# Turning q and k of four heads together, with their loads, a tile's regions and an order table

## The chip, the cores and the metric

The kernel runs on one core of a Trainium2 chip. Its engines run side by side, each through its own instructions in order: TensorE (PE, with the loading of its stationary operand shown apart as PEld), VectorE (DVE), ScalarE (ACT), GpSimd (POOL), SyncE (SP). Here POOL issues most DMAs, those that turn float32 into bf16 among them, and SP the others. The metric is the device time of one execution in microseconds; three runs of the kernel before give a median of 296.29 us (295.89 to 300.01).

## The reference

Attention with one added to the softmax's denominator, over 8 batches of 12 heads (448 tokens, head width 64), then a soft mixture of experts (8 experts, 4 slots each, hidden width 1024):

```python
scores = scale * np.matmul(q, k.transpose(0, 1, 3, 2))
m = np.max(scores, axis=-1, keepdims=True)
e = np.exp(scores - m)
attn = e / (np.sum(e, axis=-1, keepdims=True) + np.exp(-m) + 1e-09)
x = np.matmul(attn, v)            # then heads side by side: x is (3584, 768)
logits = x @ phi                  # (3584, 32)
d = softmax of logits over the rows;  c = softmax of logits over the 32 slots
slot_input = d.T @ x
slot_out[e] = np.maximum(slot_input[e] @ w1[e], 0) @ w2[e]
out = c @ slot_out
```

## The kernel before

Work goes by pairs of heads: 48 pairs, n = 0 to 47, six to a batch. The 448 rows of a pair's scores are four tiles, i = 0 to 3; the last, of 64 rows, holds both heads. The main loop has a slot s per pair, of two halves (y = 0, 1; hs = 2s + y). The steps, with the letter that the order strings use:

- `load` (L168): DMAs by POOL of q, k (six heads, 336 KB each) or v (two issues) into `nq0`/`nq1` and `nv`.
- T: `T(n)` (L241) turns q and k of a pair: 28 transposes of 64x64, one head in rows 0 to 63 and the other in rows 64 to 127, into a PSUM buffer of pool psB; one copy, by ACT (L263) or DVE (L265), takes it to a tile `qk0` to `qk6`.
- a: `A` (L274) computes scores with queries in the partitions (L285, L304) into psA, and DVE takes row maxima (L287, L307). It runs some pairs ahead.
- `W1` (L310, POOL) lays the negated maxima of three pairs out, `W2` (W, L332, PE) turns them and `W3` (ACT) evacuates them.
- B: `Bk` (L352) computes scores with keys in the partitions (s, L367), adds the maxima (b, L370), and ACT takes the exponentials (L372) into one of the `e2` tiles. The letters behind B0, B1, B2 (`assbba`) are the order in which score, bias and `A`'s score matmuls of the two heads are issued. B3 (L393, L396) is tile 3, whose matmuls use a 64x64 part of the array.
- V: `AV` (L418) multiplies exponentials and v (L433), query tiles 0 to 2; H is the fourth, 8 matmuls of 64 columns of stationary operand each.
- N: `N1` (L440) evacuates this to `ubuf`; M: `N2` (L449) makes the denominators (DVE) and divides (POOL, L466 to L477), into `x0` or `x1` by batch.
- X: `PX(n)` (L491) turns 128 columns of x (L498), ACT evacuates (L504) to `xTa`/`xTb`.
- `V(g)` (L403): POOL brings v of six heads into the layout `vp0`/`vp1` that AV reads (L405 to L408).
- P: steps of `P(b)` (L513) for a finished batch: logits (`l_mm`, L532), maxima, exponentials, slot sums (`s_mm`, L620), at half slots listed in `post`.

Up to slot 2 the order is the string `ramp`; from 3 to 41 it is `order[s % 6]`; from 42 on the code below it. PE, ACT, DVE and POOL run in the order in which these steps are issued. Pool psB has four PSUM buffers (T, B, W2, PX), psA three (A, P), psV one (AV).

One big tile `W` holds the weights. Its first 11 parts stay; the part behind (`R`, `at_`) holds the regions named above and takes the last 40 rows of weights when they are free: `rows_at` (L694) says at which half slot up to which row is loaded. Some rows are brought to DRAM as bf16 earlier (`stage_at`), and SP fetches them. After the last slot POOL also fills `spread` and `own4` (L868 to L875), behind its last row loads.

Of the kernel before, what the change touches and what calls it, by code (L numbers as in the profile page):

```python
# [31 lines left out]
def kernel(  # L32
# [47 lines left out]
    NQK, NE, VPN, NATV = 7, 5, HG * 4 * VS, HG * 4 * D  # L80
    sizes = [("nq0", 2 * NP * S), ("nq1", 2 * NP * S), ("nv", NATV), ("qk6", 2 * S), ("wm1", 512),
             ("qk0", 2 * S), ("qk1", 2 * S), ("qk2", 2 * S), ("wm0", 512), ("xTa", 4 * 512), ("qk3", 2 * S),
             ("vp0", VPN), ("x0", 4 * DD), ("qk4", 2 * S), ("qk5", 2 * S), ("e2", NE * 2 * S), ("e1", S),
             ("vp1", VPN), ("xTb", 2 * 512), ("x1", 4 * DD)]
# [72 lines left out]
    with ExitStack() as at:  # L157
# [9 lines left out]

        def load(g, nm, l0=0, l1=NP):  # L168


            b, h0 = g // 2, (g % 2) * HG
            src = {"q": q, "k": k, "v": v}[nm][b, h0:h0 + HG]
            if nm != "v":
                t = part(f"nq{g % 2}", "qk".index(nm) * NP * S, NP * S).rearrange("p (l x) -> p l x", l=NP)
                x = src.rearrange("(l h) (j t) d -> (h j) l (t d)", h=2, t=7)
                gdma(out=t[:, l0:l1, :], in_=x[:, l0:l1, :])
# [8 lines left out]
        raw = w_tile(10)[:, 0:4 * S].bitcast(F32).rearrange("p (a x) -> p a x", a=2)  # L185
        for a, src in enumerate((q, k)):
            nc.sync.dma_start(out=raw[:, a, :], in_=src[0, 0:2].rearrange("h (j t) d -> (h j) (t d)", t=7))
# [26 lines left out]
        first_qk = [part(f"nq0", a * NP * S, NP * S).rearrange("p (l x) -> p l x", l=NP)[:, 0, :] for a in range(2)]  # L214
        nc.scalar.copy(first_qk[0], raw[:, 0, :])  # L215
        nc.vector.tensor_copy(first_qk[1][:, 0:4 * D], raw[:, 1, 0:4 * D])
        nc.scalar.copy(first_qk[1][:, 4 * D:S], raw[:, 1, 4 * D:S])
# [23 lines left out]
        def T(n):  # L241
            g, pl = divmod(n, NP)
            first = n < NP * NP
            ps = psB.tile([128, 2, S], BF16, tag="b", name="ps_t")

            k0 = [psB.tile([128, 2, S], BF16, tag="b", name="ps_k") for _ in range(2)] if n == 0 else None
            for a in range(2):
                src = nat["qk"[a], g]
                order = [(tok, hl) for tok in range(7) for hl in range(2)]
                if a and n == 0:  # L250
                    order.sort(key=lambda z: kcol(z[1], z[0]))
                for tok, hl in order:
                    c = kcol(hl, tok) if a else (2 * tok if tok < 4 else 2 * tok - 7) * 64
                    r = slice(64 * hl, 64 * hl + 64)
                    o = k0[c // 256][r, 0, c:c + 64] if a and n == 0 else ps[r, a, c:c + 64]
                    nc.tensor.transpose(o, src[r, pl, tok * D:(tok + 1) * D], ident[r, r])  # L256
            t = qk_t[n % NQK]
            if n == 0:
                nc.scalar.copy(t[:, 0, :], ps[:, 0, :])
                nc.vector.tensor_copy(t[:, 1, 0:256], k0[0][:, 0, 0:256])  # L260
                nc.vector.tensor_copy(t[:, 1, 256:S], k0[1][:, 0, 256:S])
            elif first or n % 6 in (0, 3):
                nc.scalar.copy(t, ps)  # L263
            else:
                nc.vector.tensor_copy(t, ps)  # L265
            qkT[n] = t

# [132 lines left out]

        def V(g):  # L403
            t, s = vp[g % 2], nat["v", g]
            nc.gpsimd.tensor_copy(t[:, 0:HG:2, 0:3, 0:D], s[:, 0:HG:2, 1:4, :])  # L405
# [43 lines left out]
        def N2(n):  # L449
# [10 lines left out]
            else:  # L460
# [3 lines left out]
            c = pb * 128  # L464
            rec2 = psm.tile([128, 2], F32, tag="rec2", name="rec2", bufs=3)
            eng.tensor_mul(  # L466
                x[:, 0:3, c:c + 128].rearrange("p i (h d) -> p i h d", h=2),
                u[:, 0:6, 0:D].rearrange("p (i h) d -> p i h d", h=2),
                rec[:, 0:6].rearrange("p (i h) -> p i h", h=2).unsqueeze(3).to_broadcast([128, 3, 2, D]))
            if n == NPAIR - 1:  # L470
# [7 lines left out]
                x[:, 3, c:c + 128].rearrange("p (h d) -> p h d", h=2),  # L478
# [197 lines left out]
        for z in range(3):  # L676
            post.setdefault(2 * NPAIR - 5 + 2 * z, []).append(last[z])
# [11 lines left out]
        for _ in range(22):  # L689
# [4 lines left out]
        rows_at = {77: 3, 83: 7, 85: 12, 89: 17, 91: 20, 92: 24, 93: 26, 95: 27}  # L694
# [15 lines left out]
        wait_loads = []  # L710
        waits = [r for z in stage_at.values() for y in z for r in range(*y)]
        def slot_loads(s):
            g = (s + 10) // 3
            if s == 1 or (s and s % 3 == 2):
                if g < NG:
                    load(g, "q")
                    load(g, "k")
            g = (s + 9) // 3
            if s % 3 == 0 and g - 2 < NG - 1:
                V(g - 2)  # L720
                if s and g - 1 < NG:
                    load(g - 1, "v")

        ramp = ("T0 A A T1 A A W0 T2 A G0 A X0 J0 A B0.0 A B0.1 A A T3 A B0.2 A A T4 C0.3 V0.0 W1 A V0.1 V0.2 A X1 T5 "
                "A B1.0 A K0 Y2 K1 D0 V0.3 H0 C1.1 N0 B1.2 A T6 C1.3 V1.0 V1.1 A B2.0 M0 A T7 B2.1 A V1.2 V1.3 W2 T8 "
                "H1 A N1 B2.2 V2.0 X2 C2.3 Z0 V2.1 M1 K2 ")
        for word in ramp.split():
# [17 lines left out]
            elif op == "N":  # L747
                N1(*arg)
            elif op == "M":
                N2(*arg)  # L750
            elif op == "G":
                V(0)
                load(1, "v")
                ones_in(vp[1], nc.gpsimd)
            elif op == "J":
                for nm in "qk":
                    load(2, nm)
                load_half(0, 0, w_tile(0))
            elif op == "D":
                load_half(0, 1)  # L760
            elif op == "Y":
                load(2, "v")
                if 1 in half_at:
                    load_half(half_at[1], 0, w_tile(half_at[1]))
            elif op == "Z":
                PX(0)
            elif op == "K":
                slot_loads(*arg)
        for s in range(3, NPAIR + 1):
            for y in range(2):  # L770
                hs = 2 * s + y
                if s < NPAIR - 6:
                    for word in order[s % 6][y].split():
# [8 lines left out]
                        elif op == "T":  # L782
                            T(s + 6)
# [6 lines left out]
                        elif op == "X":  # L790
                            PX(s - 2)
# [4 lines left out]
                else:  # L796
# [18 lines left out]
                    else:  # L815
# [3 lines left out]
                        if s < NPAIR:  # L819
                            for i in (0, 1):  # L820
                                AV(s, i, range(3))
                    for f in post.get(hs, ()):
                        f()
                    if y and 0 <= s - 2 < NPAIR - 2:
                        PX(s - 2)
# [12 lines left out]
                if y == 0 and s and s + 1 in firsts:  # L838
                    W1(mg(s + 1))
                if y == 0 and wait_loads:  # L840
                    f, z = wait_loads.pop()
                    f(z)
                if y == 0 and s % 3 == 2 and (s + 1) // 3 < NG:
                    if s == NPAIR - 4:
                        V(NG - 1)
                    if s - 1 in half_at:
                        load_half(half_at[s - 1], 0, w_tile(half_at[s - 1]))
                if y == 0 and s - 1 in stage_at:
                    stage_rows(*stage_at[s - 1][0])
                if y == 0 and s - 2 in half_at:  # L850
                    load_half(half_at[s - 2], 1)
                if y == 0 and s - 2 in stage_at:
                    stage_rows(*stage_at[s - 2][1])
# [3 lines left out]
            if s > 2 and s + 2 in firsts:  # L857
                wait_loads.append((slot_loads, s))
            else:
                slot_loads(s)  # L860
            if 2 * s + 1 in rows_at:

                if 2 * s + 1 == 89:
                    load_rows(7, 9)
                load_rows(rows + 2 * (rows == 7), rows_at[2 * s + 1])
# [200 lines left out]
```

## Time and profile before

| what | value |
|---|---|
| three runs, median (lowest, highest) | 296.29 us (295.89, 300.01) |
| the profiled execution | 295.49 us |
| its span, first to last instruction | 293.7 us |
| PE busy | 270.2 us (92%) |
| DVE busy | 249.7 us (85%) |
| ACT busy | 249.0 us (85%) |
| POOL busy | 196.3 us (67%) |
| chain of waits, PE's share | 77% |
| granted TensorE clock, mean | 0.961 |
| q, k DMAs (336 KB), issue to landing, median | 6.4 and 7.2 us |

Busy time of an engine is that of its instructions with overlaps counted once. Matmuls overlap each other, so what one costs is read from the starts of two groups that follow each other, not from its length. The granted clock is full until the output stage after 265 us.

### The profile page before, as it was taken

The page shows a single profiled execution, that of the slowest core. Times are in us where ns is not written, and L with a number is a line of the kernel's source. Part 1 is how long each engine was busy: PE and PEld are TensorE (multiplying, and loading weights), DVE is VectorE, ACT ScalarE, POOL GpSimd, SP SyncE. Part 2 cuts the span into 40 slices and gives each one's busy share as a digit, 9 for nine tenths or more (in the row PEclk, how much of TensorE's full clock was granted, in tenths as well). Part 3 has the DMA queues.
Part 4 walks back from the last instruction along what each step waited for, and adds up shares of the span by engine and source line. Part 5 has one row for each costly group of instructions (what it writes and reads, how often), then busy time and mean ns, then how long its engine had stood idle before and what let it go on. Part 6 is the DMA issues. An engine that isn't in the chain of part 4 may idle for free.

```text
span 293.7 us, 12399 instructions
## 1 busy us (share of the span) xinstructions
PE 270.2 (92%) x5174; PEld 156.9 (53%) x5174; DVE 249.7 (85%) x581; ACT 249.0 (85%) x559; POOL 196.3 (67%) x391
## 2 busy tenths in 40 slices
PE   5999999999999999999999999999999999995810
PEld 4445555565665566565655665556555556652100
DVE  5999799999999989999999999999999565537920
ACT  4569999999999999999999999999999986337810
POOL 8786677889787978897888879887975823000000
PEclk9999999999999999999999999999999999999555
DMA  7999997999999999999999999999989999809997
GB/s 134 150 148 196 175 145 121 196 185 187 187 192 163 199 177 205 180 193 186 198 176 194 188 185 177 191 181 199 155 132 208 197 210 274 303 4 345 382 444 328
DMA packets 47016, 58.67 MB, mean 200 GB/s; under 512 B 2801, under 2 KB 39921, under 8 KB 46705
## 3 DMA queue, kind: packets, MB, share of 16 engines
q0 software_dynamic: 40304, 42.29, 90.7%
q1 hardware_dynamic: 6656, 15.60, 14.0%
q8 instruction: 40, 0.66, 0.8%
q14 instruction: 16, 0.12, 0.1%
HBM read 89.16 MB, written 15.14 MB: 355 GB/s over the span
## 4 chain that ended last, share of the span: by engine, by line
PE 77%; ACT 8%; DVE 4%; POOL 3%; issue 2%; DMA 1%; DVEq 0%; POOLq 0%; ACTq 0%
PE ps_av L433 16%; PE ps_b L367 10%; PE ps_a L285 10%; PE ps_t L256 8%; PE ps_b L370 7%; PE ps_b L393 4%; PE ps_x L498 4%; PE ps_b L396 3%; ACT W L399 2%; PE ps_s L620 2%; PE ps_o L959 2%; DVE mx L298 2%; PE ps_h L896 2%; PE ps_l L532 2%; PE ps_a L294 2%
## 5 line engine op out<-in xcount | busy, mean ns | idle before, releaser
L287 DVE TENSOR_REDUCE mx<-ps_a 128x1 f32<-128x448 f32 x250 | 139.1, 611 | 3.2 <-PE ps_a L285 2.4
L372 ACT ACTIVATE W<-ps_b 128x448 bf16<-128x448 f32 x250 | 125.0, 576 | 4.1 <-PE ps_b L370 3.3
L285 PE MATMUL ps_a<-W 64*128 64x448 bf16 x250 | 82.7, 354 | 0.0
L433 PEld LDWEIGHTS <-W 128*128 128x128 bf16 (+1 forms) x1536 | 53.9, 100 | 34.9 <-issue 31.1
L433 PE MATMUL ps_av<-W 128*128 128x65 bf16 (+1 forms) x1536 | 70.7, 196 | 0.6 <-ACT ubuf L446 0.6
L367 PE MATMUL ps_b<-W 64*128 64x448 bf16 x250 | 65.8, 355 | 0.0
L370 PE MATMUL ps_b<-mT,sel 64*128 64x448 bf16 x250 | 64.6, 350 | 0.0
L466 POOL TENSOR_TENSOR W<-ubuf,rec 128x384 bf16<-128x384 f32 x44 | 36.5, 829 | 27.5 <-DVE rec L462 14.5
L399 ACT ACTIVATE W<-ps_b 128x448 bf16<-128x448 f32 x86 | 46.5, 580 | 2.3 <-PE ps_b L396 2.0
L256 PEld LDWEIGHTS <-W 64*64 64x64 bf16 x1344 | 26.7, 112 | 17.5 <-issue 14.7
L256 PE MATMUL ps_t<-ident,W 64*64 64x64 bf16 x1330 | 31.2, 197 | 1.4 <-ACT W L215 1.4
L504 ACT CAST W<-ps_x 128x512 bf16<-128x512 f32 x47 | 29.6, 631 | 1.2 <-PE ps_x L498 1.0
L307 DVE TENSOR_REDUCE mx<-ps_a 128x1 f32<-128x448 f32 x48 | 29.6, 616 | 0.6 <-PE ps_a L304 0.6
L114 POOL DMA_DIRECT2D W<-in_moe_w_dram x30 | 22.7, 756 | 7.9 <-PE ps_b L396 7.7
L393 PE MATMUL ps_b<-W 64*64 64x448 bf16 (+1 forms) x134 | 26.8, 368 | 0.3
L285 PEld LDWEIGHTS <-W 64*128 64x128 bf16 x250 | 22.5, 94 | 7.8
L396 PE MATMUL ps_b<-mT,sel 64*64 64x448 bf16 (+1 forms) x134 | 25.4, 357 | 0.1
L370 PEld LDWEIGHTS <-sel 64*128 64x128 bf16 x250 | 20.7, 94 | 8.0 <-issue 2.7
L446 ACT COPY ubuf<-ps_av 128x455 f32<-128x455 f32 x44 | 24.4, 555 | 0.0
L263 ACT COPY W<-ps_t 128x896 bf16<-128x896 bf16 x21 | 19.7, 939 | 5.5 <-PE ps_t L256 5.5
L298 DVE TENSOR_REDUCE mx<-ps_a 128x1 f32<-128x448 f32 x38 | 21.1, 616 | 1.5 <-PE ps_a L294 1.5
L477 POOL TENSOR_TENSOR W<-ubuf,rec 128x128 bf16<-128x128 f32 x44 | 17.5, 398 | 3.7
(156 smaller groups left out, 446.6 us busy)
## 6 DMA issues: line engine op xcount, KB each, us to landing
W<-in_moe_w_dram POOLq DMA_DIRECT2D x24, 768.0 KB, 9.4
W<-in_v_dram POOLq DMA_DIRECT2D x32, 192.0 KB, 6.7
out_dram<-W SPq DMA_DIRECT2D x2, 2688.0 KB, 10.5
W<-in_q_dram POOLq DMA_DIRECT2D x15, 336.0 KB, 6.4
W<-in_k_dram POOLq DMA_DIRECT2D x15, 336.0 KB, 7.2
stage<-in_moe_w_dram POOLq DMA_DIRECT2D x4, 768.0 KB, 9.4
W<-stage SPq DMA_DIRECT2D x4, 576.0 KB, 6.9
out_dram<-W SPq DMA_DIRECT2D x6, 384.0 KB, 3.1
```

The costliest lines, as they stand in the source:

```text
L256: nc.tensor.transpose(o, src[r, pl, tok * D:(tok + 1) * D], ident[r, r])
L285: nc.tensor.matmul(ps[:, 0:S], t[r, 0, i * 128:(i + 1) * 128], t[r, 1, :], start=True, stop=True)
L287: nc.vector.reduce_max(m[:, c:c + 1], ps[:, 0:S], axis=AX.X)
L307: nc.vector.reduce_max(mx[g][:, c:c + 1], ps[:, 0:S], axis=AX.X)
L367: nc.tensor.matmul(pss[hl][:, 0:S], t[rs[hl], 1, cols], t[rs[hl], 0, :], start=True, stop=False)
L370: nc.tensor.matmul(pss[hl][:, 0:S], sel[rs[hl], 2 * pl + hl:2 * pl + hl + 1].to_broadcast([64, 128]), mT[mg(n)][rs[hl], :], start=False, s ...
L372: nc.scalar.activation(e[:, hl, :], pss[hl][:, 0:S], AF.Exp, scale=scale)
L393: nc.tensor.matmul(outs[hl], t[rs[hl], 1, cols], t[rs[hl], 0, :], start=True, stop=False)
L396: nc.tensor.matmul(outs[hl], sel[rs[hl], 2 * pl + hl:2 * pl + hl + 1].to_broadcast([64, m]), mT[mg(n)][rs[hl], :], start=False, stop=True)
L399: nc.scalar.activation(e, p[:, 0:S], AF.Exp, scale=scale)
L433: nc.tensor.matmul(o, eT[n, i, hl][:, qc], vp[g % 2][:, 2 * pl + hl, i, 0:W65], start=(i == 0 and u == 0 and hl == 0) or (u == 3 and i == ...
L466: eng.tensor_mul(x[:, 0:3, c:c + 128].rearrange("p i (h d) -> p i h d", h=2), u[:, 0:6, 0:D].rearrange("p (i h) d -> p i h d", h=2), rec[: ...
```

## The change

Four heads at a time: from pair 6 to pair 45 `T4(j, a)` turns q (a = 0) or k (a = 1) of pairs 2j and 2j + 1 with 14 transposes of 128 partitions x 64 columns, and one copy writes the halves into two neighbouring `qk` tiles, of which there are now eight. `load4(j)` loads q and k of four heads (224 KB each) into `raw`, which holds four pairs' places; the load of j + 2 is issued after j is turned. The pairs hold other heads for this (4m + h and 4m + 2 + h), so v's places, the columns written by `N2` and the time of `PX` (s - 3 instead of s - 2) change with them.

```diff
-    NQK, NE, VPN, NATV = 7, 5, HG * 4 * VS, HG * 4 * D
-    sizes = [("nq0", 2 * NP * S), ("nq1", 2 * NP * S), ("nv", NATV), ("qk6", 2 * S), ("wm1", 512),
...
+    NQK, NE, VPN, NATV = 8, 5, HG * 4 * VS, HG * 4 * D
+    two = lambda i: [(f"qk{i}", 2 * S), (f"qk{i + 1}", 2 * S)]
+    sizes = [("raw", 8 * S), ("wm1", 512)] + two(0) + [("nv", NATV)] + two(2) + [("xTa", 4 * 512), ("wm0", 512)] + \
+            two(4) + [("x0", 4 * DD)] + two(6) + [("free", 2 * S), ("e2", NE * 2 * S), ("e1", S), ("vp0", VPN), ("vp1", VPN),
+                                                  ("xTb", 2 * 512), ("x1", 4 * DD)]
...
+        four = lambda n: PB <= n < NPAIR - 2
+
+        def load4(j):
+            b, m = divmod(j, 3)
+            for a, x in enumerate((q, k)):
+                x = x[b, 4 * m:4 * m + 4].rearrange("(l h) (j t) d -> (h j) l (t d)", h=2, t=7)
+                gdma(out=raw[a][:, 2 * (j % 2):2 * (j % 2) + 2], in_=x)
...
+        def T4(j, a):
+            n = 2 * j
+            turned[j] = turned.get(j, 0) + 1
+            if j > 3 and turned[j] == 2 and j + 2 < NPAIR // 2:
+                wanted.append(j + 2)
+            if not four(n):
+                T(n + a)
+                return
+            ps = psB.tile([128, 2, S], BF16, tag="b", name="ps_t")
+            for tok in range(7):
+                for l in range(2):
+                    c = kcol(l, tok) if a else (2 * tok if tok < 4 else 2 * tok - 7) * 64
+                    nc.tensor.transpose(ps[64 * l:64 * l + 64, :, c:c + 64], raw[a][:, (n + l) % 4, tok * D:(tok + 1) * D],
+                                        ident)
+            cp = nc.scalar.copy if (n + a) % 6 in (0, 3) else nc.vector.tensor_copy
+            o = at_[f"qk{n % NQK}"] + a * S
+            cp(R[:, o:o + 4 * S].rearrange("p (h x) -> p h x", h=2)[:, :, 0:S], ps)
...
+            if g >= 2:
+                runs = [(0, slice(0, 3, 2), slice(0, 2), 0), (1, slice(1, 2), slice(0, 2), 1)]
...
+                for hl, a, c, at in runs:
...
+                    nc.gpsimd.tensor_copy(o[:, :, :, 0:3, 0:D], z[:, :, :, 1 - hl:4 - hl, :])
+                    nc.gpsimd.tensor_copy(o[r, :, :, 3, 0:D], z[r, :, :, 3 * hl, :])
...
-            post.setdefault(2 * NPAIR - 5 + 2 * z, []).append(last[z])
+            post.setdefault(2 * NPAIR - 5 + 2 * z + (z == 0), []).append(last[z])
...
-        rows_at = {77: 3, 83: 7, 85: 12, 89: 17, 91: 20, 92: 24, 93: 26, 95: 27}
+        rows_at = {79: 1, 83: 7, 86: 9, 88: 14, 89: 15, 91: 17, 92: 21, 93: 22, 95: 25}
...
-        order = (("P V2 B0assbba V3 B1sabsba",
-                  "H N B2ssbaba T B3 P V0 V1 X M"),
-                 ("V2 P B0assbba V3 B1saasbb",
-                  "H P N B2assbba T B3 V0 V1 X M"),
-                 ("V2 B0assbba P V3 B1assbba",
-                  "H N B2asasbb B3 T W P V0 V1 M X"),
-                 ("B0assbba P V2 V3 H N B1ssabba T",
-                  "M B2sasbba B3 X V0 P V1"),
-                 ("B0assbba T B1sasbba P V2 V3 H",
-                  "N B2assbab B3 V0 P M X V1"),
-                 ("B0assbba V2 V3 P B1sabsab H N",
-                  "B2ssbaab T B3 P V0 W V1 M X"))
+        order = (("V2 V3 B0asbsba H B1assbba N P",
+                  "Q B2sabsab M X V0 P V1 B3"),
+                 ("B0asbsba V2 V3 B1assbba P K",
+                  "H N P B2sabsab B3 M V0 V1 X"),
+                 ("B0ssabba X V2 V3 B1assbba P H N",
+                  "B2sabsab P W V0 V1 M B3"),
+                 ("B0asbsba V2 B1assbba V3 P",
+                  "H N Q P K X M V0 B2sabsab V1 B3"),
+                 ("B0asbsba V2 B1assbba P V3 H N Q",
+                  "B2sabsab B3 V0 M V1 P X"),
+                 ("V2 B0ssabba V3 B1assbba P H K",
+                  "N B2sabsab P B3 V0 W X V1 M"))
+        px_at = {84: 39, 87: 40, 88: 41, 91: 42, 92: 43, 94: 44, 95: 45}
...
-                "A B1.0 A K0 Y2 K1 D0 V0.3 H0 C1.1 N0 B1.2 A T6 C1.3 V1.0 V1.1 A B2.0 M0 A T7 B2.1 A V1.2 V1.3 W2 T8 "
-                "H1 A N1 B2.2 V2.0 X2 C2.3 Z0 V2.1 M1 K2 ")
+                "A B1.0 A K0 Y2 L4 D0 V0.3 H0 C1.1 N0 B1.2 A Q3.0 C1.3 V1.0 V1.1 A B2.0 M0 A Q3.1 B2.1 A V1.2 V1.3 W2 "
+                "H1 A N1 B2.2 V2.0 X2 C2.3 V2.1 M1 L5 ")
...
+                        elif op == "Q":
+                            T4((s + 6 - s % 2) // 2, 0)
+                        elif op == "K":
+                            T4((s + 4 + s % 2) // 2, 1)
...
-                            PX(s - 2)
+                            PX(s - 3)
...
+                if (c, y) in ((1, 0), (4, 0)) and (s + 2) // 3 < NG:
+                    V((s + 2) // 3)
+                if y == 0:
+                    if s % 3 == 2 and s + 1 in firsts:
+                        W1(mg(s + 1))
+                    if c % 3 == 2 and (s + 4) // 3 < NG:
+                        load((s + 4) // 3, "v")
+                while wanted:
+                    load4(wanted.pop())
```

In the ramp J0 loads with `load4(3)`, L is `load4`, Q is `T4`, and K0 is `V(1)`; Z0 was `PX(0)`. In the order strings Q turns q and K turns k. `c` in the last piece is s % 6. The loads of weight halves move from the middle of a slot to its end. L367, L370, L336, L498, L532, L620 of before are L400, L403, L369, L551, L585, L673 of after; the new transposes are L295.

More of the change, by code (lines that the diff above doesn't have):

```diff
@@ L166 @@
         ubuf = pu.tile([128, 2, 7 * W65], F32, name="ubuf")
+        raw = [R[:, 4 * a * S:4 * (a + 1) * S].rearrange("p (l x) -> p l x", l=4) for a in range(2)]
+        extra = [w_tile(9)[:, a * NP * S:(a + 1) * NP * S].rearrange("p (l x) -> p l x", l=NP) for a in range(2)]
+        four = lambda n: PB <= n < NPAIR - 2
[4 more added lines that the diff above has]
+                gdma(out=raw[a][:, 2 * (j % 2):2 * (j % 2) + 2], in_=x)
+        turned, wanted = {}, []
         def load(g, nm, l0=0, l1=NP):
@@ L182, in load @@
             nat[nm, g] = t
[L185 removed]
+        f32 = w_tile(10)[:, 0:4 * S].bitcast(F32).rearrange("p (a x) -> p a x", a=2)
         for a, src in enumerate((q, k)):
[L187 removed]
+            nc.sync.dma_start(out=f32[:, a, :], in_=src[0, 0:2].rearrange("h (j t) d -> (h j) (t d)", t=7))
         make_identity(nc, ident)
@@ L213 @@
         nc.vector.memset(ones[64:128, 1:2], 0.0)
[L214 to L217, printed above, removed]
+        nc.scalar.copy(raw[0][:, 0, :], f32[:, 0, :])
+        nc.vector.tensor_copy(raw[1][:, 0, 0:4 * D], f32[:, 1, 0:4 * D])
+        nc.scalar.copy(raw[1][:, 0, 4 * D:S], f32[:, 1, 4 * D:S])
         for h in range(2):
@@ L266, in T @@
             qkT[n] = t
+        def T4(j, a):
[15 more added lines that the diff above has]
+            cp(R[:, o:o + 4 * S].rearrange("p (h x) -> p h x", h=2)[:, :, 0:S], ps)
+            for h in range(2):
+                qkT[n + h] = qk_t[(n + h) % NQK]
         firsts = [0, 1] + list(range(3, NPAIR, 3))
@@ L755 @@
             elif op == "J":
-                for nm in "qk":
-                    load(2, nm)
+                load4(3)
                 load_half(0, 0, w_tile(0))
+            elif op == "Q":
+                T4(*arg)
+            elif op == "L":
+                load4(*arg)
             elif op == "D":
@@ L856 @@
                     rows = rows_at[hs]
[L857 to L860, printed above, removed]
             if 2 * s + 1 in rows_at:
-                if 2 * s + 1 == 89:
-                    load_rows(7, 9)
-                load_rows(rows + 2 * (rows == 7), rows_at[2 * s + 1])
+                load_rows(rows, rows_at[2 * s + 1])
                 rows = rows_at[2 * s + 1]
```

76 lines of the change are left out of this document (34 added, 42 removed).

## The prediction

> **What bounds the kernel now.** I read the chain of waits first: TensorE (PE) holds 77% of it, and from 37 to 229 us it is PE work in which the same pieces return every 28.7 us. That is six slots; a slot handles one pair of heads. Next I took the busy time of each engine in one such period (the next one takes 28.82).
>
> ```profile
> core 0: us, PE busy (x) PEld busy (x) DVE busy (x) ACT busy (x) POOL busy (x), PEclk, DMA share, GB/s
> 116.67:145.28 28.61, 28.61 (x604) 17.29 (x598) 27.70 (x65) 27.93 (x66) 24.55 (x49) 1.00 1.16 190
> ```
>
> PE (its weight loads, PEld, run beside it) never rests, and three other engines are close behind. ACT and DVE overlap the ends of their instructions, so their true floor is lower. Three lines of the chain of waits show it, and show POOL:
>
> ```profile
> 11.75 3.19 DVE mx L298 x6
> ...
> 92.02 0.81 POOL W L176
> ...
> 101.72 0.40 POOL W L477
> ```
>
> Six maxima back to back take 3.19, so 0.53 each, not the 0.61 of the groups. A period has 42 maxima (22.3), 4 evacuations of turned q and k on DVE (2.1), 6 denominators (0.31 each, 1.9) and some 1.3 of slot statistics: DVE floor 27.6, or 1.1 us under PE. For ACT the same gives about 26.6 (exponentials stand 0.42 to 0.44 apart). POOL, at 24.6 of 28.7, was the chain itself from 92.0 to 101.7.
>
> PE's prices, from its timeline (start, length, line, count):
>
> ```profile
> 100.01 0.32 PE L433 MATMUL ps_av<-W 128*64 128x65 bf16 x8
> 100.26 0.36 PE L367 MATMUL ps_b<-W 64*128 64x448 bf16 x2
> ...
> 100.94 0.56 PE L256 MATMUL ps_t<-ident,W 64*64 64x64 bf16 x24
> ...
> 101.88 0.35 PE L433 MATMUL ps_av<-W 128*128 128x65 bf16 x6
> 102.62 0.34 PE L336 MATMUL ps_m<-ident,W 128*128 128x128 bf16 x3 [0.39 <-POOL W L314]
> ...
> 103.00 0.39 PE L498 MATMUL ps_x<-ident,W 128*128 128x128 bf16 x4
> 103.23 0.34 PE L433 MATMUL ps_av<-W 128*128 128x65 bf16 x6
> ```
>
> Read starts, not lengths. PX: 4 matmuls of 128 columns in 0.23, 57 ns each, so a column streams in 0.44 ns. A score block (100.26 to 100.94) is three streams of 448 columns, 0.19 each, plus 0.11: that is what a change of the array's tile (128x128, 64x128, 64x64, 128x64) costs. Turn of a pair plus B3, both 64x64: 100.94 to 101.88, 0.94. Elsewhere the two stand alone:
>
> ```profile
> 37.45 0.63 PE L256 MATMUL ps_t<-ident,W 64*64 64x64 bf16 x28
> 38.01 0.36 PE L367 MATMUL ps_b<-W 64*128 64x448 bf16 x1
> ...
> 40.20 0.38 PE L393 MATMUL ps_b<-W 64*64 64x448 bf16 x2
> ...
> 40.70 0.36 PE L433 MATMUL ps_av<-W 128*128 128x65 bf16 x6
> ```
>
> A turn alone costs 0.56 and B3 alone 0.50; next to B3 the turn costs 0.94 - 0.50 = 0.44.
>
> **Turning four heads, on PE.** The instruction order of before has, per period, four turns beside B3 and two alone: 4x0.44 + 2x0.56 = 2.88. The change has 84 instead of 168 transposes per period, each of 128 columns on a 128x64 tile. Unknown is whether two of them, on the two column halves, stream together. The nearest rows say yes: the eight L433 on 128x64 tiles take 0.25 with a tile change of 0.11, 17 ns each for 65 columns that alone need 29. So 42 streams x 57 ns = 2.40, and as only one of the six half-turns has a run of its own (the others join the AV pieces of that tile), 0.11 more: 2.51. But AV pieces that were joined are now apart: 15 runs of 128x128 for 13, +0.22. Sum -0.15 a period; 40 turned pairs are 6.7 periods: **-1.0**. Half as many transposes is thus nearly nothing, since columns, not instructions, are paid. If they streamed singly: 42x57 ns = +2.4 a period, +16.
>
> [...]
>
> **Evacuations.** As many copies as before; in the steady part the same third on ACT. The written tiles lie apart by a stride; no row shows that, the copies of equal size are 0.53 (DVE) and 0.79 (ACT) apart, and I take no difference (0 to +0.1 each, 40 copies, mostly under PE).
>
> **Ramp.** ACT runs without a gap from 24 to 37 us; the timeline of ACT has T7's copy at 29.21 and T8's here:
>
> ```profile
> 35.02 1.01 ACT L263 COPY W<-ps_t 128x896 bf16<-128x896 bf16 x1
> 35.80 1.11 ACT L372 ACTIVATE W<-ps_b 128x448 bf16<-128x448 f32 x2
> ```
>
> T7's copy goes to DVE, T8's leaves the ramp, PX(0) is put off: 2x0.79 + 0.47 = 2.05 less on ACT. DVE has three gaps of 0.4 to 0.6 there, enough for one more copy (0.53), and PE saves T8's 0.56. I take **-1.5**, ends -2.0 and 0.
>
> **POOL and loads.** q and k loads go from 34 issues to 48; in a period from 4 to 6, 2x0.79 = +1.6, POOL 24.6 to 26.2 of 28.7. Bytes and packet sizes stay. Behind them on POOL stand N2 and W1. V (2x0.66 + 2x0.35 = 2.0) now stands at the middle of slots 1 and 4 of six. From there to W1 in slot 2: V 2.0, two issues 1.6, N2 1.5, W1 0.8, together 5.9 for the 4.8 of a slot. V may start ahead of its place (it waits for no PE work there, and slot 0 has 2.3 us on POOL), and W2 asks 0.8 after. Taken at nothing, with 0 to 1.6 a period for the range. PX is a slot later, which gives N2 room. A load has over two slots (10 us) to land against medians of 6.4 and 7.2 us: covered.
>
> **Order table.** The six streams of a score block still alternate row halves in every new string, so no stream is lost. Where two half-turns and PX follow each other (slot 3) three of the four psB buffers go in a row: 0 to 0.5 a period, taken as 0.
>
> **Tail.** The deferred PX adds 0.47 of ACT, near full from 230 to 245. PX(41) now stands directly ahead of P(6)'s 24 logit matmuls; before, 2.1 us lay between (226.81 to 228.91). Twenty of the 24 cover 0.5 of an evacuation that needs 0.6 plus an exponential ahead of it: 0.3 to 1.0. Together **+1.0** (0 to 1.5). The last rows now wait for the exponentials' tiles, freed at about 245.9 instead of 243.9; behind that issue on POOL stand `spread` and `own4` (2.4 us), so ready near 249, while DVE asks for `own4` at 250.0: nothing, but only 1 us is left.
>
> **Sum:** -1.0 - 1.5 + 1.0 = -1.5. The profiled execution took 295.49 (span 293.7 and 1.8 around it), the median is 296.29: 294.0 in its terms, **294.8** as a median.
>
> **Rivals.** About 2% (5.9 us; under 290.4, over 302.2) is what a measurement can tell here.
> - POOL decides (slower): its added issues push W1 late, PE waits at W2 and N2 follows. For: the chain of 92 to 101.7, and L336 already waited 0.39 for L314. Against: that is the only one of its kind in the run. At half to all of 1.6 a period: +5 to +11, 300 to 306; over 2% from 1.1 us of wait a period. Chance 0.22.
> - Buffers of psB or psA run dry in the new order: 0.5 to 1.2 a period, 298 to 303. For: PE, DVE and ACT are within 4%. Against: before has no such wait. 0.12.
> - [...] 0.05.
> - PE saves more than I found and DVE's floor binds: -1.1 x 6.7 and the whole ramp, 286 to 290. Against: the PE sum. 0.07.
> - My forecast, 290.5 to 299: 0.54.
>
> Slower by over 2%: three quarters of the first (0.165), half of the second, the third: 0.28. Faster: 0.06. Within: 0.66. Range **290 to 306**: it leaves out 0.06 below, and the top of POOL's case and most of the third above.
>
> **What would show it.** After: the period still 28.5 to 28.7; 28 new transposes per four heads starting in pairs 57 ns apart; POOL near 26.2 a period and no wait of L369 on POOL; the copies of turned tiles as long as now; everything from slot 3 on 1 to 2 us earlier; a PE wait at P(6)'s logits. A period of 29.7 or more with PE waiting would make the forecast wrong, as would transposes 57 ns apart singly.

## The result, and the profile after

| | before | after |
|---|---|---|
| median (lowest to highest) | 296.69 us (295.89 to 300.01), 20 runs | 297.83 us (296.96 to 298.85), 20 runs |
| the profiled execution, its span | 295.49, 293.7 us | 298.12, 296.3 us |

The ratio after to before is 1.0028, 95% interval 1.0015 to 1.0041: 0.8 us slower by the ratio, where 1.5 us faster was forecast. Small, but on the other side of zero.

To see where it lies I cut both profiled executions at the same events: the first exponential of pairs 0, 6, 18 and 42, the end of the last exponential, the first matmul of the hidden layer, the first slot matmul, the first and the last issue of an output, its landing, the end. Two experiments that are told below stand beside them.

| stretch, us | before | after | e_wide | e_best |
|---|---|---|---|---|
| start to pair 0 | 12.29 | 12.64 | 12.83 | 12.58 |
| pair 0 to 6 (ramp) | 34.48 | 34.82 | 33.98 | 33.91 |
| pair 6 to 18 | 57.36 | 57.64 | 57.64 | 57.65 |
| pair 18 to 42 (four periods) | 114.88 | 114.14 | 114.13 | 114.15 |
| pair 42 to the last exponential | 26.27 | 26.75 | 26.75 | 26.75 |
| to the hidden layer | 6.00 | 6.07 | 6.07 | 6.07 |
| to the first slot matmul | 5.92 | 6.42 | 5.93 | 5.93 |
| to the first output issue | 6.49 | 6.66 | 6.47 | 6.48 |
| to the last output issue | 17.24 | 17.70 | 17.40 | 17.70 |
| to its landing | 11.83 | 12.16 | 11.60 | 11.32 |
| to the end | 0.91 | 1.27 | 1.28 | 0.91 |

The span grew by 2.6 us, more than the medians did, since the profiled execution of before was a quick one. Some rows scatter from execution to execution: the start was 12.24 to 12.83 over the changed kernels, and the output stage is taken up at the end. So the rows show where time goes, and the ratio how much. The regular part did get shorter. What it won was lost in the tail and, 1.87 us of it, behind the last pair, where the change edits next to nothing.

The regular part first. The busy time of the engines in one period of after, pairs 18 to 24, and in the same period of before (columns as ahead):

```profile
core 0: us, PE busy (x) PEld busy (x) DVE busy (x) ACT busy (x) POOL busy (x), PEclk, DMA share, GB/s
105.10:133.55 28.45, 28.45 (x509) 16.71 (x507) 27.71 (x65) 28.10 (x65) 26.19 (x50) 1.00 1.17 192
```

```profile
104.13:132.75 28.62, 28.62 (x593) 17.31 (x591) 27.70 (x65) 27.92 (x66) 24.07 (x47) 1.00 1.16 188
```

PE is still what never rests, with 84 matmuls fewer and 0.17 us less. POOL is at 26.2, as forecast, and stays off the path here. The next period of before, pairs 24 to 30, takes 28.91: pair 29 takes 4.93 there and 4.65 one period earlier. No wait in the profile explains that, and the change has no part in it. The price of a turn is seen in PE's timeline of after, where a half-turn has a run of its own:

```profile
95.96 0.61 PE L483 MATMUL ps_av<-W 128*128 128x65 bf16 x14
96.40 0.56 PE L295 MATMUL ps_t<-ident,W 128*64 128x128 bf16 x14
96.89 0.36 PE L400 MATMUL ps_b<-W 64*128 64x448 bf16 x1
```

From start to start 0.49: a tile change of 0.10 and 14 transposes in 0.39, 28 ns each. They start in seven pairs, 3 ns apart in a pair and 56 ns from pair to pair, where one of PX's transposes, of 128 columns too, takes 57: here the two column halves run side by side.

In the second period, pairs 12 to 18, POOL is the path, however. The chain of waits of after, just ahead of pair 18:

```profile
96.56 0.39 PE ps_t L295 x14
...
97.70 0.76 POOL W L114
98.46 0.69 POOL acc L657
99.15 0.77 POOL W L452
...
99.97 0.40 POOL W L453
...
100.43 0.50 POOL W L452
...
101.36 0.83 POOL W L519
...
102.54 0.40 POOL W L530
...
103.44 0.34 PE ps_m L369 x3
```

Before had such a chain at 92.0 to 101.7. From the first exponential of pair 17 to that of 18 it now takes 5.49 us, at the same place of the next period 4.67: 0.82 lost; before it was 5.20 against 4.65, 0.55 lost. Of it PE shows 0.31 as a wait for DVE's copy of cT at 100.32, and 0.2 between the end of the AV pieces (102.94 and 0.29) and L369.

In the ramp PE's timeline of after has a wait for the load of pairs 10 and 11:

```profile
38.26 0.60 PE L483 MATMUL ps_av<-W 128*128 128x65 bf16 x14
39.60 0.58 PE L295 MATMUL ps_t<-ident,W 128*64 128x128 bf16 x14 [0.74 <-DMA W<-in_q_dram]
```

Its issue stands on POOL at 34.09. The stretch of the ramp in which ACT had no gap, 24 to 37 us, in before and then in after:

```profile
24.00:37.00 13.00, 12.31 (x261) 7.46 (x262) 11.31 (x26) 13.00 (x29) 7.71 (x15) 1.00 1.14 184
```

```profile
24.00:37.00 13.00, 12.81 (x202) 7.08 (x202) 12.47 (x28) 12.08 (x27) 8.01 (x17) 1.00 1.02 165
```

ACT now has room (12.08 busy of 13.00). But PE had stood idle there for only 0.69 us, and that fell to 0.19. And behind the last pair, PE's timeline of after and then of before, the first 72 matmuls of the hidden layer:

```profile
252.06 4.56 PE L940 MATMUL ps_h<-W,ubuf 128*32 128x512 bf16 x72
```

```profile
251.28 4.07 PE L896 MATMUL ps_h<-W,ubuf 128*32 128x512 bf16 x72
```

The same work takes 0.49 longer. Instruction by instruction it is one hole behind the 38th of them, and the list of waits of after has only this for it:

```profile
PEld L940 <- issue: 0.6, 1, 0.6
```

"Issue" means that PE waited for nothing that the profile shows. Ahead of the hole the instruction queue moved 16 KB, from 252.04 to 253.05; the hole ends at 254.5.

### The profile page after: what moved, and what is told of

Its sections match the earlier page's. It is cut to its first block, busy times and chain, and to the rows that moved or that the text cites. A ratio compares the mean times of both kernels' runs of the same rounds, so it can differ in the third digit from the quotient of the medians.

```text
span 296.3 us, 11266 instructions
## 1 busy us (share of the span) xinstructions
PE 270.7 (91%) x4614; PEld 153.3 (52%) x4614; DVE 251.1 (85%) x583; ACT 249.4 (84%) x557; POOL 206.3 (70%) x409
## 4 chain that ended last, share of the span: by engine, by line
PE 74%; ACT 7%; DVE 6%; DMA 3%; POOL 2%; issue 2%; DVEq 0%; SPq 0%; POOLq 0%; ACTq 0%
PE ps_av L483 16%; PE ps_a L318 9%; PE ps_b L400 9%; PE ps_b L403 7%; PE ps_t L295 5%; PE ps_b L426 5%; PE ps_x L551 4%; DVE mx L331 4%; PE ps_b L429 3%; PE ps_o L1003 3%; ACT W L432 2%; PE ps_h L940 2%; PE ps_s L673 2%; DMA W<-in_q_dram 2%; PE ps_a L327 2%
## 5 line engine op out<-in xcount | busy, mean ns | idle before, releaser
L405 ACT ACTIVATE W<-ps_b 128x448 bf16<-128x448 f32 x250 | 122.1, 559 | 3.2 <-PE ps_b L400 0.9
L318 PE MATMUL ps_a<-W 64*128 64x448 bf16 x250 | 85.6, 354 | 0.4 <-DVE cT L678 0.3
L483 PE MATMUL ps_av<-W 128*128 128x65 bf16 (+1 forms) x1536 | 72.2, 196 | 0.1
L403 PE MATMUL ps_b<-mT,sel 64*128 64x448 bf16 x250 | 67.5, 349 | 0.0
L400 PE MATMUL ps_b<-W 64*128 64x448 bf16 x250 | 66.6, 355 | 0.0
L432 ACT ACTIVATE W<-ps_b 128x448 bf16<-128x448 f32 x86 | 45.2, 566 | 2.8 <-PE ps_b L429 2.6
L318 PEld LDWEIGHTS <-W 64*128 64x128 bf16 x250 | 23.3, 93 | 14.7 <-issue 7.6
L557 ACT CAST W<-ps_x 128x512 bf16<-128x512 f32 x47 | 28.5, 605 | 0.6 <-PE ps_x L551 0.6
L403 PEld LDWEIGHTS <-sel 64*128 64x128 bf16 x250 | 23.5, 95 | 6.2 <-issue 1.0
L295 PE MATMUL ps_t<-ident,W 128*64 128x128 bf16 x560 | 21.5, 220 | 0.7 <-DMA W<-in_q_dram 0.7
L295 PEld LDWEIGHTS <-W 128*64 128x64 bf16 x560 | 16.7, 110 | 6.3 <-issue 5.5
L452 POOL COPY W<-W 128x384 bf16<-128x384 bf16 (+1 forms) x29 | 19.0, 656 | 0.9
```

What stands on the lines that cost most here:

```text
L295: nc.tensor.transpose(ps[64 * l:64 * l + 64, :, c:c + 64], raw[a][:, (n + l) % 4, tok * D:(tok + 1) * D], ident)
L318: nc.tensor.matmul(ps[:, 0:S], t[r, 0, i * 128:(i + 1) * 128], t[r, 1, :], start=True, stop=True)
L400: nc.tensor.matmul(pss[hl][:, 0:S], t[rs[hl], 1, cols], t[rs[hl], 0, :], start=True, stop=False)
L403: nc.tensor.matmul(pss[hl][:, 0:S], sel[rs[hl], 2 * pl + hl:2 * pl + hl + 1].to_broadcast([64, 128]), mT[mg(n)][rs[hl], :], start=False, s ...
L405: nc.scalar.activation(e[:, hl, :], pss[hl][:, 0:S], AF.Exp, scale=scale)
L432: nc.scalar.activation(e, p[:, 0:S], AF.Exp, scale=scale)
```

## The experiments

**Is the tail only scatter?** The kernel before, unchanged, once more.

> The kernel before, unchanged, for a second profile. Theory R (part of the 2.6 us between the two profiled spans is the scatter of single executions, and sits in the code behind the last attention pair, which both kernels share): the stretch from the first matmul of the hidden layer (251.28 in the first profile) to the end of the span, 42.4 us there and 44.2 in the changed kernel, comes out anywhere from 42.4 to 44.2. Rival: that stretch is 42.4 +- 0.3 for this kernel always, and the changed kernel's later loads make it longer.

296.82 us (295.8 to 298.33) beside 296.49, ratio 1.0011 (0.9984 to 1.0037). From the hidden layer to the end it took 42.6 us, where before took 42.4; after took 44.2, as do the next three kernels. So the loss behind the last pair belongs to the changed program. It is steady: from the start of the hidden layer to the last landing before took 41.5 and 41.7, the changed kernel and four variants told below 42.9 to 43.0.

**The late load, and the place of PX.** e_early5 sends load4(5) directly behind load4(4) into a spare place of a weight tile; e_px moves PX(40) and PX(41) one half slot forward; e_both does the two.

```diff
-  "A B1.0 A K0 Y2 L4 D0 ...      ... V2.1 M1 L5 "
+  "A B1.0 A K0 Y2 L4 L5 D0 ...   ... V2.1 M1 "
```

```diff
-  px_at = {84: 39, 87: 40, 88: 41, ...}
+  px_at = {84: 39, 86: 40, 87: 41, ...}
```

> The changed kernel, with load4(5) put into a free part of the weight tile and issued right behind load4(4) in the ramp, instead of behind the ramp's last step. Theory L (the ramp's gain is given back because this load comes late: issued at 34.09, landed at 39.56, PE waits 0.74 at 39.60 for it): no wait of the new transposes on a DMA, PE's work from slot 4 on 0.6 to 0.8 us earlier, time 297.2 to 297.4 against 297.83 (ratio to the kernel before about 1.000). Rival M (PE's wait is filled anyway, since the deferred turn and the evacuations are what is late at slots 3 to 5): the wait goes, the time stays at 297.8 (ratio 1.002 to 1.004).

> The changed kernel, with PX(40) and PX(41) one half slot earlier (half slots 86 and 87 instead of 87 and 88), so that PX(41) no longer stands directly ahead of the logits of batch 6. Theory of my tail term (the logits wait 0.3 to 1.0 us for that evacuation): 0.3 to 1.0 us faster than the changed kernel, 296.8 to 297.5. Rival (ACT is the bound there, and the order of PE's waits behind it does not matter): within 0.2 us of 297.83.

> Both edits: load4(5) early, and PX(40), PX(41) a half slot earlier. If both waits are on the path the gains add: 1.0 to 1.6 us under the changed kernel, 296.2 to 296.8, ratio to the kernel before 0.998 to 1.000. If neither is, 297.8.

e_early5: 297.3 us, ratio 1.0014 (0.9997 to 1.0031), 0.4 us under the change, though the two intervals overlap. PE's timeline of it shows the wait gone:

```profile
38.18 0.60 PE L485 MATMUL ps_av<-W 128*128 128x65 bf16 x14
38.62 0.56 PE L297 MATMUL ps_t<-ident,W 128*64 128x128 bf16 x14
```

Pair 0 to 6 fell from 34.82 to 33.99. e_px: 297.57 us, ratio 1.0032 (1.0009 to 1.0054), nothing gained, pair 42 to the last exponential 26.84 for 26.75: the place of PX(41) was not the cost. In after the wait at P(6)'s logits is 0.20, as PE's timeline has it:

```profile
229.65 0.66 PE L585 MATMUL ps_l<-phi_sb,W 128*128 128x32 bf16 x20
230.50 0.27 PE L585 MATMUL ps_l<-phi_sb,W 128*128 128x32 bf16 x4 [0.20 <-ACT W L557]
```

e_both: 297.38 us, ratio 1.0021 (1.0004 to 1.0039), not told apart from e_early5. Its profile is no help for the ramp: the granted clock was at half from 18.08 to 21.49, and pairs 0 to 3 took 21.29 instead of 19.66.

**What the hole is.** e_wide replaces each four filler matmuls of 64 columns by one of 256.

```diff
-  for _ in range(4 * n):
-      nc.tensor.matmul(st["idle"][:, 0:64], ident, w_sb["w1", 0][:, 0, 0:64], start=True, stop=True)
+  for _ in range(n):
+      nc.tensor.matmul(st["idle"][:, 0:256], ident, w_sb["w1", 0][:, 0, 0:256], start=True, stop=True)
```

> The changed kernel with each four filler matmuls of 64 columns (ahead of the hidden layer) replaced by one of 256: 48 matmuls and 48 weight loads fewer in the program, the same streaming time. The trace of the change has a hole of 0.48 us in the hidden layer that no instruction explains and that ends 1.4 us after a 16 KB transfer of instructions. Theory F (TensorE runs dry of instructions there): 96 instructions fewer move that boundary to a later place, where matmuls take longer each; the hole goes or shrinks below 0.25, hidden layer to first slot matmul from 6.42 to 5.9 to 6.1 us, 0.4 to 0.9 us off (output stage included): 296.9 to 297.4. Rival W (the hole is a weight or a transfer that comes late): the hole stays at the same group of matmuls with 0.4 to 0.5, time 297.8.

295.96 us (295.63 to 297.25), ratio 0.9986 (0.9970 to 1.0002): 1.2 us better than the change by the ratios, more than theory F gave, and as fast as before. PE's timeline of e_wide:

```profile
251.40 4.07 PE L940 MATMUL ps_h<-W,ubuf 128*32 128x512 bf16 x72
```

The hole is gone, though the late weights landed as late as in after (259.7 and 260.0 us). None of the seven profiles with wide fillers has it. All six of the change with the old fillers have, always behind the 38th matmul: 0.49, 0.82, 0.88, 0.49, 0.52 and 1.10 us. Each ends 1.4 to 1.5 us behind a 16 KB transfer of instructions, in e_sem too, where all this comes 13 us later. The hole isn't all that the wide fillers take away: from the start of the hidden layer to the last landing it is 41.4 in all six profiles of the changed kernel that have them, 1.5 less than in after. Why the outputs land later by more than the hole stays open.

The mirror images on the kernel before: b_pad adds 160 PE instructions in the tail, b_wide has the wide fillers.

```diff
+  for _ in range(16 if 41 <= n < 46 else 0):
+      nc.tensor.matmul(pss[0][:, 0:1], ident, ident[:, 0:1], start=True, stop=True)
```

> The kernel before, with 16 matmuls of one column (overwritten by the next) ahead of each of the transposes of pairs 41 to 45: 160 instructions of TensorE more, which puts the instruction boundary at the place, counted from the hidden layer, where the changed kernel has it. Theory F: a hole of 0.3 to 0.7 us appears in the hidden layer, which had none: 5.92 to 6.3 to 6.6 us; together with what the added matmuls cost in the slots themselves (0 to 1 us, read off the stretch from pair 42 to the last exponential) 0.4 to 1.8 us slower. Rival W: no hole, hidden layer to first slot matmul 5.9, and only the slots' own 0 to 1 us.

> The kernel before, with the wide filler matmuls alone. It has 96 instructions of TensorE fewer, which are all ahead of the hidden layer, so that (10247 and 9223 instructions, both 7 over a multiple of 256) the boundary of the 16 KB transfers now stands where the changed kernel had it. Theory F1 (the place of the boundary alone makes the hole): a hole of 0.3 to 0.6 us in the hidden layer that before did not have, 296.8 to 297.4 beside 296.45. Theory F2 (it takes the boundary and the 80 short instructions of the fillers just ahead, which use up what was fetched): no hole, hidden layer to first slot matmul 5.9 to 6.0, time 296.2 to 296.7. Either way the fillers have no gain of their own for a kernel without the hole; a gain of over 0.8 us here would mean that they cost time by themselves.

b_pad took 300.37 us, ratio 1.0113 (1.0072 to 1.0155), but the execution that was profiled took 1,208.8 us, so the cost of the added matmuls and a hole can't be separated. The time is higher than either theory allowed, and the run decides nothing; a hole made at will is thus missing. b_wide took 297.54, ratio 1.0020 (0.9988 to 1.0053), with no hole in the hidden layer (5.93): the fillers gain nothing for a kernel without it. Whether the place of the boundary alone makes the hole it doesn't settle, for its transfers don't start where those of after do: 115 PE instructions ahead of the hidden layer and 139 behind its start, in after right at it. But its profile has such a hole elsewhere, in a turn of the old kind, which is as dense (28 transposes in 0.56):

```profile
152.75 0.44 PE L256 MATMUL ps_t<-ident,W 64*64 64x64 bf16 x16
153.71 0.38 PE L256 MATMUL ps_t<-ident,W 64*64 64x64 bf16 x12 [0.53 <-issue]
```

There, too, a 16 KB transfer of instructions ended shortly ahead (152.08). The likely reading is this: PE ran out of instructions where many short ones follow each other, and the change moved that point onto 40 fillers and the hidden layer, because it has 1,120 PE instructions fewer. Shown is that in the changed kernel the fillers' form decides over the hole, and that it follows a transfer; that PE ran dry is argued from these two.

**The last waits.** e_sem sends the late rows 17 to 21 at one place (row 21 joins 17 to 20, not 22 as the expectation has it), which makes one DMA of SyncE less.

```diff
-  rows_at = {..., 92: 21, 93: 22, 95: 25}
+  rows_at = {..., 92: 22, 95: 25}
```

> The changed kernel with rows 21 and 22 of the late weights sent together instead of in two pieces, so SyncE issues one DMA fewer, as many as before the change. Theory E (the last waits): after the last output has landed SyncE works off a list of some twenty semaphore waits of 60 ns each, and the one DMA more puts the last output's semaphore six places earlier in it; so the stretch from the last landing to the end goes from 1.27 us back to about 0.9, and nothing else moves: 0.36 us off, 297.4 to 297.5 beside 297.8. Rival: the list has nothing to do with the number of DMAs; the stretch stays at 1.27 and the time at 297.8.

310.19 us, ratio 1.0462 (1.0430 to 1.0494). Row 21 lies over q of pair 46, and at place 92 the second half of its scores is still to come: in this kernel those scores are made from weights, and PE waits until they have landed. From the list of waits, and PE's clock in two stretches:

```profile
PE ps_b L426 <- DMA W<-stage: 10.4, 1, 10.4
```

```profile
core 0: us, PE busy (x) PEld busy (x) DVE busy (x) ACT busy (x) POOL busy (x), PEclk, DMA share, GB/s
245.00:250.00 5.00, 0.00 (x0) 0.00 (x0) 0.00 (x0) 0.00 (x0) 0.00 (x0) 0.50 0.83 223
250.00:255.00 5.00, 4.80 (x41) 1.96 (x42) 0.00 (x0) 2.31 (x6) 0.00 (x0) 0.50 0.01 3
```

The wait of 10.4 cost 12.3, for PE came back at half clock. One thing could still be read: from the last landing to the end it was 1.33, not 0.9. With 24, 25 and 26 DMAs of SyncE it is 0.91, 1.33 and 1.27. The records of SyncE in the three traces show why: it ends with the same list of waits for semaphores in the same order, some 60 ns each, and behind the wait that the last output ends, 0, 7 and 6 of this list are left. That is as if the semaphores were handed out eight in turn. e_best tests it.

**The evacuation more in the tail.** e_px2 sends PX(38) and PX(39) one slot earlier each; e_px3, run later on top of e_best, only PX(39).

```diff
   elif op == "X":
-      PX(s - 3)
+      if s < 41:
+          PX(s - 3)
+      if s > 39:
+          PX(s - 2)
```

> The changed kernel with the transposes PX(38) and PX(39) each one slot earlier (slots 40 and 41 of the regular part), so that the tail has as many transposes as before the change. Theory T (the 0.49 us that the stretch from pair 42 to the last exponential grew is the one evacuation of 0.47 more on ACT): that stretch falls from 26.75 to 26.2 to 26.4, while the period of pairs 36 to 42 grows by 0 to 0.25; 0.25 to 0.5 us off, 297.3 to 297.6. Rival: the tail grew for another reason (POOL's rows, the order of the logits); the stretch stays at 26.7 to 26.85.

e_px2 took 301.49 us, ratio 1.0157 (1.0126 to 1.0188). A turn of four puts heads 4 and 6 into one pair, 5 and 7 into the next, so PX(38) needs N2 of both. PE's timeline, and its clock right after:

```profile
215.13 0.34 PE L551 MATMUL ps_x<-ident,W 128*128 128x128 bf16 x3 [2.10 <-POOL W L519]
215.88 0.29 PE L551 MATMUL ps_x<-ident,W 128*128 128x128 bf16 x1 [0.41 <-POOL W L530]
```

```profile
215.00:220.00 5.00, 4.46 (x64) 2.27 (x64) 2.40 (x4) 2.48 (x6) 0.91 (x4) 0.66 0.07 11
```

2.5 us of waiting took 4.4, since PE then ran 3.4 us at half clock.

> The mended kernel with PX(39) already in slot 41 behind PX(38) (both need N2(38) and N2(39), which are done by then, since the four heads of a turn lie across two columns blocks of x), so that the tail has one evacuation less on ACT. Theory T (the tail's 0.49 us is this evacuation): pair 42 to the last exponential falls from 26.75 to 26.25 to 26.35, pairs 36 to 42 take 0 to 0.25 longer; 295.1 to 295.5. Rival: the tail grew for another reason and stays at 26.7 to 26.85.

e_px3: 295.48 us, ratio 0.9970 (0.9950 to 0.9989), no such wait. The tail fell from 26.75 to 26.49 (in e_px2 to 26.48), pairs 36 to 42 grew from 28.79 to 29.26. So about half of the tail's 0.48 is that evacuation, and it costs 0.47 where it was put; the other half stays open.

**All mends together.** e_best is the change with the load of e_early5, the wide fillers, and SyncE's DMAs cut from 26 to 24 where no place is in use.

```diff
-  rows_at = {..., 89: 15, 91: 17, 92: 21, ...}
+  rows_at = {..., 89: 15, 92: 21, ...}
-  fetch_rows(35, 37)
-  fetch_rows(37, 40)
+  fetch_rows(35, 40)
```

> The changed kernel with three edits: the wide fillers; load4(5) issued in the ramp into a spare place; SyncE's DMAs cut from 26 to 24 (row 16 with 17 to 19, rows 35 and 36 with 37 to 39), which, if the last waits are handed out over 8 semaphores in turn (24 DMAs before the change: 0.92 us from the last landing to the end; 26: 1.27; 25: 1.33), puts the last output last in the list again. By these theories: pair 0 to pair 6 at 33.9 to 34.3 us, hidden layer to first slot matmul 5.9, last landing to end 0.9; 295.2 to 295.8, ratio 0.996 to 0.998. Rival: rows 15 and 16 half a slot later and the merged transfers come too late for the second layer: a wait for them there, 295.9 or more.

> The mended kernel once more, as the base for e_pool on the same chip: 295.3 to 295.8 and pair 17 at 5.5 us again, if the first measurement holds.

295.53 us (295.12 to 295.77), ratio 0.9950 (0.9926 to 0.9973); again, on another occasion, 295.37, ratio 0.9951 (0.9925 to 0.9977). Each mend shows in its own row of the table, 0.91 from the last landing to the end included. This is 1.5 us faster than before by the ratio, the number that the forecast had for the change. That is luck: ramp, regular part and tail make 0.5 of it by the table (-0.57, -0.44 and +0.48), and the fastest runs, 295.12 and 295.67, differ by as much. The rest is that the runs of before scatter more. One place of it may be pairs 24 to 30, which took 28.91 and 29.07 in its two profiles, and 29.92 in b_wide, where a hole stands.

**POOL in the second period.** e_pool gives N2(16) to DVE; e_half sends one half of a weight tile behind W1 of slot 17 instead of ahead of it. Both on top of e_best.

```diff
-  on_pool = lambda n: n < NPAIR - 4
+  on_pool = lambda n: n < NPAIR - 4 and n != 16
```

```diff
-  if s - 2 in half_at:
+  if s - 2 in half_at and s != 15:
       load_half(half_at[s - 2], 1)
   ...
+  if s == 17:
+      load_half(half_at[13], 1)
```

> The mended kernel (e_best) with N2(16), three POOL instructions that take 1.5 us on POOL ahead of W1 in the second period, given to DVE. Theory P (in that one period POOL is the chain: it stands still for 1.15 us ahead of the load issue at 96.2, and V, N2 and W1 behind it come late, which is why pair 17 takes 5.50 us where the same place takes 4.67 in every later period): pair 17 falls to 4.7 to 4.9, DVE takes the work in the time that it now waits, and the run is 0.6 to 0.8 us shorter than e_best: 294.7 to 295.0. Rival: the place is bound by something else that is late with POOL (the cT copy on DVE, the turned tiles), or DVE now makes the others wait; pair 17 stays over 5.2, the time at 295.3 or more.

> The mended kernel (e_best) with one half of a weight tile (one issue, 0.77 us on POOL) sent behind W1 of the second period instead of ahead of V, N2 and W1. Theory P (POOL is the chain there): W1 stands 0.77 earlier, pair 17 falls from 5.49 to 4.7 to 4.8 us, the run is 0.6 to 0.8 shorter than e_best: 294.6 to 294.9. Rival: something else is late together with POOL; pair 17 stays over 5.2, the time at 295.3 to 295.6.

e_pool was the wrong step: N2(16) stands behind W1, the one ahead of it is N2(15). It took 296.44 us, ratio 0.9998 (0.9974 to 1.0022); pair 17 took 5.74 and pair 18 5.61 instead of 5.50 and 4.77. DVE's timeline, then two waits of PE's:

```profile
104.40 0.56 DVE L521 TENSOR_TENSOR W<-ubuf,rec 128x384 bf16<-128x384 f32 x1
104.87 0.22 DVE L531 TENSOR_SCALAR rec<-halfm,rec 128x2 f32<-128x2 f32 x1
105.13 0.29 DVE L532 TENSOR_TENSOR W<-ubuf,rec 128x128 bf16<-128x128 f32 x1
```

```profile
102.52 0.35 PE L485 MATMUL ps_av<-W 128*128 128x65 bf16 x6 [0.51 <-DVE ubuf L498]
...
106.01 0.35 PE L320 MATMUL ps_a<-W 64*128 64x448 bf16 x1 [0.58 <-DVE mx L322]
```

1.07 us of work on DVE made the run 1.1 us longer than e_best again: DVE has no room there.

e_half does what theory P says at the place: pair 17 takes 4.73 instead of 5.48. But the issue that was moved lands among others, the next load of v comes at 127.07, and V, behind it on POOL, waits for that (the profile names PE, which was long done):

```profile
127.22 0.82 POOL L454 COPY W<-W 128x768 bf16<-128x768 bf16 x1 [1.38 <-PE ps_b L402]
```

Pair 23 takes 5.85 instead of 4.67, and the whole is no faster: 295.94 us, ratio 0.9971 (0.9941 to 1.0000). So POOL's chain is the cause at pair 17, shown, and a remedy that only moves an issue moves the stall.

## Why the prediction was wrong, point by point

- **Turning four heads, on PE: right.** -0.15 a period was the sum; the four regular periods gave -0.17, -0.46, -0.08 and -0.04. The second holds the loss of before at pair 29, so that some 0.5 of the 0.74 is the change's. 14 transposes in 0.39 are the 28 ns each that the paired price gives. Their weight loads, 110 ns each, ran beside them: from pair to pair it was 56 ns, and the run of 14 shows no wait.
- **Evacuations: right in size, not quite at nothing.** The copies last 0.62 on DVE and 0.92 on ACT as before. Once, at 50.65, PE waited 0.24 for one of them.
- **POOL and loads, "taken at nothing": wrong in one period.** POOL's chain at pair 17 lost 0.82 where it had lost 0.55. With the wait of 0.24 this is most of why pairs 6 to 18 got 0.28 longer, while the same two periods were to bring -0.3. The rival in which POOL decides everywhere fell: L369 waited for POOL once in the regular part, for 0.2, and once in the tail, for 0.22.
- **Ramp, "-1.5": the step that failed, and the largest miss.** It grew by 0.34 in the profile. ACT's 2.05 less was priced as if ACT alone held the ramp, but PE had only 0.69 of idle time to lose from 24 to 37 us. Two mistakes more: "PE saves T8's 0.56" counts a turn as saved that is only put off to slot 3; without the wait, pairs 0 to 3 won 0.85 and pairs 3 to 6 gave 0.26 back, so 0.5 to 0.6 was there. And "a load has over two slots (10 us) to land: covered" doesn't hold in the ramp: load4(5) is issued at 34.09 and its turn was ready at 38.86, 4.8 us later against a landing of 5.5. Its wait is 0 to 0.8 from run to run; e_early5 removes it.
- **Tail, "+1.0": right in sign, twice too large.** 0.48. The deferred evacuation is there, the logits' wait is 0.20 where 0.3 to 1.0 was taken.
- **What was left out: all that lies behind the last pair.** The sum gave it nothing, since the change edits little there. But in a program that is 1,120 PE instructions shorter the 16 KB transfers of instructions came at other places: in after one started at 252.04, where the hidden layer does (252.06); in before the nearest ones started 3.45 ahead of it (247.83) and 2.43 behind its start (253.71). And after, which issues two DMAs more, had 6 waits of SyncE's list left behind the last output, before 0. Of the 1.87 us the hole is 0.49 in this profile and the last waits are 0.35; most of the rest is the later landing of the outputs, which went with the wide fillers and whose cause is open. That the hole hangs on the fillers' instructions is shown by e_wide, which touches neither data nor order; that the last waits turn over with the count of DMAs by e_best.
- **"What would show it".** The period, the pairs of transposes, POOL's 26.2 and the logits' wait came as written (the period with 28.45, just under the 28.5 named, and 28.78 in the last); "everything from slot 3 on 1 to 2 us earlier" did not: pair 6 started at 47.46 instead of 46.77.
- The last rows, `spread` and `own4`: their issue on POOL ran at 247.1, and nobody waited for `own4`. The rivals of dry buffers and of single streaming fell with the regular periods, 28.45 to 28.78. The third rival, which the sum of chances counts with 0.05, no run shows: in after no weight load held up the new transposes, which stood 56 ns apart in pairs.

Open: what POOL waits for in the 1.15 us ahead of the load at 96.22 (the profile names PE, as it did where it was a load), half of the tail's 0.48, what before loses at pair 29, and why the outputs land later where the hole is.

## What to carry to other kernels

Work that is put off is not work that is saved: follow it to its new place before it enters the sum, and check a load's lead time in the ramp and not only in the regular part. When a change removes or adds instructions by the hundred, or only a DMA or two, look also at code that it doesn't touch: here a hole of 0.49 to 1.10 us came up among dense short instructions, and a few wide fillers in place of many narrow ones closed it (the 72 matmuls took 4.07 instead of 4.56), at 295.96 us instead of 297.83. A wait of PE can cost more than its length: in e_px2 2.5 us cost 4.4, since the clock halved behind it.

## What the runs showed of the hardware that was not expected

- The instruction queue moved 16 KB at a time, in 0.88 to 1.38 us: 40 times in before, with 10,348 matmuls and weight loads, and 36 times in after, with 9,228. By these counts, as an estimate, one transfer goes with 256 to 259 of PE's instructions. In dense code a hole of 0.49 to 1.10 us ended 1.4 to 1.5 us behind one (all six profiles of the change with its own fillers).
- The clock halved for 3.4 us behind an idle time of PE of 2.5 us (e_px2) and for 13.7 us around one of 10.4 (e_sem), but not behind one of 0.74 (after). The longest wait alone doesn't tell it: in e_both it halved at 18.08, where the longest wait was 0.69 and PE had been busy for 2.37 of the 3.42 us ahead; after, with 2.76 of 3.41 at the like place, kept its clock. What decides is not shown.
- Stretches at one clock lasted 3.41 us (e_both), 13.65 (e_sem) and 256.00 (before and after), which is 1, 4 and 75 times 3.41. In the output stage the clock fell 6.9, 6.3, 5.5, 4.4 and 3.9 us after the first output was issued, and the stage up to the last issue took 17.24, 17.40, 17.44, 17.70 and 17.71 (before, e_wide, e_px, after, e_early5). Half a microsecond of that row is chance and not the change, and it doesn't reach the end: with 17.24 (e_pool) and with 17.70 (e_best) the last output landed 41.4 us behind the start of the hidden layer.
- SyncE's last landing was followed by 0.91 us with 24 DMAs, 1.33 with 25 and 1.27 with 26.
